# Wider rows for V and its attention outputs in a fused state-space and recurrent-memory kernel

## The chip, the cores and the metric

The kernel runs on one core of a Trainium2 chip. The metric is device time in microseconds (us) from start to end of one execution. Four runs of the kernel before gave a median of 1250.6 us, from 1249.58 to 1251.2. Lower is better. TensorE is written PE, VectorE DVE, ScalarE ACT, GpSimd POOL; SP is the engine that issues most DMAs.

## The reference

Two independent layers read two inputs of 2048 x 1024 and their outputs are joined on the last axis. Part A is a state-space layer, part B a transformer layer that walks over 64 segments of 32 tokens and carries 8 memory rows from one segment to the next:

```python
def _A_ref(...):
    Bu = jnp.einsum('bld,pd->blp', x + 0j, B_bar)
    for t in range(L):
        h = Lam_bar[None, :] * h + Bu[:, t, :]
    y = 2.0 * jnp.einsum('blp,dp->bld', hseq, Cmat).real + x * Dskip
def _B_ref(...):                       # H = 32 heads of Dh = 128, M = 8, seg_len = 32
    for s in range(n_seg):
        h = jnp.concatenate([mem, xs], axis=1)
        q, k, v = (einsum('btd,dhe->bhte', h, W) for W in (Wq, Wk, Wv))
        p = _softmax(where(mask, scores, -1e9))
        o = einsum('bhqk,bhke->bhqe', p, v)
        o = einsum('bhte,hed->btd', o, Wo)
        mem = o[:, :M, :]
        outs.append(o[:, M:, :])
```

(The sketch joins lines of the reference and leaves out its arguments.)

## The kernel before

The kernel does not walk over the 64 segments one by one. It makes a guess of every segment's memory rows (lines 517 to 536), computes all segments with that guess at once, and near the end checks the guess against the memory outputs that came out (`check`, lines 794 to 847). Only if the check fails would a loop over the segments (`general`) run; with the given inputs it does not.

The work runs in four stages, with TensorE kept supplied through all of them. Stage 1 (to about 347 us) computes part A's scan and, between its matmuls, V for all tokens. V is written from PSUM to two staging tiles `b_vst` by ACT (line 490, by the helper at L87) and from there to DRAM tensors `b_vx` (line 493), one for each block of 4 heads. V of the guessed memory rows goes to `b_vt` through `v_mem` (lines 539 to 557). Stage 2 (to about 471 us) computes part A's output and the guess. Stage 3 makes Q and K for a pair of heads at a time (`proj`) and does attention (`attention`) for the pair before, interleaved; its first scores come at 486.7 us and its last outputs at 1018 us. Stage 4 multiplies the attention outputs with Wo (`outproj`), with `check` between.

For attention, 64 segments are packed into 22 groups of 3; a group has 96 token rows and 3 memory rows, 99 in all. For each of 16 pairs of heads (`hp`) and each of 11 steps `u`, `att_front` makes scores for two groups and two heads (four matmuls of 128x99 into `psS`), ACT takes the exponential, and POOL multiplies with a 0/1 mask into `b_m` (line 642). `att_back` then takes up to three blocks at a time (a block is one group and one head). For each it loads the masked weights `b_m` into PE and streams V of that group and head past them (line 656):

```python
        for i, (_, b, m, j) in enumerate(blocks):
            PE.matmul(o[:, i, :], m[:, j * GW:j * GW + 128], vt[:, b // 2, (b % 2) * EV:(b % 2 + 1) * EV], start=True, stop=True)
```

V of a head has E = 128 columns and one more of ones, so that the same matmul gives the sum of the weights: EV = 129. In the tile `b_v` (called `vt` here) a group has 2 x 129 bf16 values, the second head directly after the first, and the three outputs of one PSUM tile lie 129 fp32 values apart. DVE then takes the reciprocal of the sums (line 658) and multiplies (line 659). In the trace the outputs are `psO` and, for every third tile, `psR`. There are 16 x 44 = 704 such matmuls.

`load_v` (lines 616 to 626) fills `b_v` for a pair of heads, from `b_vx` (96 rows x 22 groups, one run of 258 values each) and `b_vt`. For the first two pairs it also fills the unused partitions 99 to 127 with zeros (line 622), read from a zero row of `b_vx` for each of 29 partitions x 22 groups. `load_v(0)` is called when stage 3 is set up (line 688), the next ones at step `u == 2` of the pair before.

Every PE and SP instruction goes through the helper `Pinned` and therefore carries line L62 in the profile; ACT and DVE copies carry L87 and L89. In stage 1 PE and SP keep the order of the program, and SP in stage 2 too; in stages 3 and 4 the framework's scheduler may move instructions on SP forward. Tiles begin on multiples of 32 bytes. The constants' pool `cst` holds `b_omT` (5120 bytes a partition), the memory outputs transposed, which `check` reads (lines 800 to 811): four transposing DMAs fill it from `b_tn`.

Of the kernel before, what the change touches and what calls it, by code (L numbers as in the profile page):

```python
# [9 lines left out]
BF16 = mybir.dt.bfloat16  # L10
# [13 lines left out]
T = 2048; D = 1024; KC = 8; TT = 16  # L24
PC = 8; TB = 512; NB = 4
H = 32; E = 128; SEG = 32; M = 8; NSEG = 64; L = M + SEG
HB = 8; HP = 16
# [3 lines left out]
NG = 22; GX = 96; GW = 99; NU = NG // 2  # L31
NSLOT = NG * GX
QW = 2208
NTL = 3 * NG
NMX = 7
NM = NTL + NMX
NR = 80
GE = 6
EV = E + 1
MW = 4 * GW + 29  # L40

XMAIN = 1920
# [9 lines left out]
class Pinned:  # L52


    def __init__(self, k, name, eng):
        self.k, self.name, self.eng = k, name, eng
# [278 lines left out]
class PartB:  # L335
    def __init__(self, k, x, mem0, Wq, Wk, Wv, Wo, out):
        self.k = k
        self.x, self.mem0, self.out = x, mem0, out
        self.Wf = [w.rearrange("(c p) h e -> p c (h e)", p=128) for w in (Wq, Wk, Wv)]
        self.Wo = Wo.rearrange("h e d -> e h d")  # L340
        self.vx = [k.drp.tile([NSLOT, 4 * EV], BF16, name=f"b_vx{i}") for i in range(HB)]
        self.vt = [k.drp.tile([NTL, 4 * EV], BF16, name=f"b_vt{i}") for i in range(HB)]
        self.on = [k.drp.tile([T, 1024], BF16, name=f"b_on{i}") for i in range(4)]
        self.tn = [k.drp.tile([NR, 1024], BF16, name=f"b_tn{i}") for i in range(4)]
        c = k.cst
        self.m0T = c.tile([128, KC, M], BF16, name="b_m0T")
        self.omT = c.tile([128, H, NR], BF16, name="b_omT")
        self.gx = c.tile([128, KC, NM], BF16, name="b_gx")
        self.vmp = c
        self.xbar = c.tile([128, KC, NSEG], BF16, name="b_xbar")  # L350
        self.ogT = c.tile([128, H, NSEG], BF16, name="b_ogT")
        self.accE = c.tile([128, HP * NU], FP32, name="b_accE")
        self.accR = c.tile([128, HP * 2 * NG], FP32, name="b_accR")
        self.flag = c.tile([1, 1], I32, name="b_flag")
# [18 lines left out]

    def fill(self, tmp):
        k = self.k
        z = tmp.tile([32, 4 * EV], BF16, name="b_xr", bufs=4)
        k.V.memset(z[:], 0.0)
        for hb in range(HB):
            k.SP.dma_start(self.vx[hb][64 + NMX:GX, :], z[0:GX - 64 - NMX, :])
            k.SP.dma_start(self.vx[hb][T + 32:NSLOT, :], z[0:32, :])  # L380
        for q in range(4):
            k.SP.dma_start(self.tn[q][NM:NR, 0:4 * EV], z[0:NR - NM, :])
            k.SP.dma_start(self.tn[q][NM:NR, 1024 - 4 * EV:1024], z[0:NR - NM, :])

    def load_x(self, q):

# [60 lines left out]
    def stage_init(self):  # L447

        self.vst = []
        for i in range(2):  # L450
            self.vst.append(self.wl.tile([128, 4, 4, EV], BF16, name=f"b_vst{i}", bufs=1))
            self.k.G.memset(self.vst[i][:, :, :, E:EV], 1.0)
        self.nst = 0

    def next_st(self):
# [160 lines left out]
    def load_v(self, hp):  # L616
        if hp < HP:
            k = self.k
            vt = self.vts[hp % 2]
            if hp < 2:  # L620
                z = self.vx[0][T + 32:T + 32 + 128 - GW, 0:2 * EV].unsqueeze(1).to_broadcast([128 - GW, NG, 2 * EV])
                k.tc.keep_in_program_order(k.SP.dma_start(vt[GW:128, :, :], z))
            hb, cs = hp // 2, slice((hp % 2) * 2 * EV, (hp % 2) * 2 * EV + 2 * EV)
            k.tc.keep_in_program_order(k.SP.dma_start(vt[0:GX, :, :], self.vx[hb].rearrange("(g p) n -> p g n", p=GX)[:, :, cs]))
            k.SP.dma_start(vt[GX:GW, :, :], self.vt[hb].rearrange("(g j) n -> j g n", j=3)[:, :, cs])
            self.vtile[hp] = vt
# [19 lines left out]
    def att_back(self, blocks):  # L646

        k = self.k; PE, V = k.PE, k.V
        hp, b0, n = blocks[0][0], blocks[0][1], len(blocks)
        vt = self.vtile[hp]  # L650
        if b0 == 0:
            self.ob = self.p3a.tile([GW, 2 * NG, E], BF16, name="b_ob", bufs=2)
        o = k.ps(("O", "O", "R")[self.nback % 3], (128, 3, EV))
        self.nback += 1
        for i, (_, b, m, j) in enumerate(blocks):
            PE.matmul(o[:, i, :], m[:, j * GW:j * GW + 128], vt[:, b // 2, (b % 2) * EV:(b % 2 + 1) * EV], start=True, stop=True)
        r = self.accR[0:GW, hp * 2 * NG + b0:hp * 2 * NG + b0 + n]
        V.reciprocal(r, o[0:GW, 0:n, E])
        V.tensor_tensor(self.ob[:, b0:b0 + n, :], o[0:GW, 0:n, 0:E], r.unsqueeze(2).to_broadcast([GW, n, E]), ALU.mult)  # L659
        q, cs = hp // 4, slice((hp % 4) * 256, (hp % 4) * 256 + 256)  # L660
        on, tn = self.on[q], self.tn[q]
        ov = self.ob[:].rearrange("p (g h) e -> p g (h e)", h=2)
        early = hp == HP - 1

        def rows(g0, g1):
            r = on[64 + GX * (g0 - 1):64 + GX * (g1 - 1), :].rearrange("(g p) n -> p g n", p=GX)
            k.SP.dma_start(r[:, :, cs], ov[0:GX, g0:g1, :])
        if early and b0 + n == 2 * GE:
            rows(1, GE)
            k.SP.dma_start(on[0:64, cs], ov[0:64, 0, :])  # L670
        if b0 + n == 2 * NG:
            del self.vtile[hp]
            if early:
                rows(GE, NG - 1)
            else:
                rows(1, NG - 1)
                k.SP.dma_start(on[0:64, cs], ov[0:64, 0, :])
            k.SP.dma_start(on[T - 64:T, cs], ov[0:64, NG - 1, :])
            k.SP.dma_start(tn[0:NTL, :].rearrange("(g j) n -> j g n", j=3)[:, :, cs], ov[GX:GW, :, :])
            k.SP.dma_start(tn[NTL:NM, cs], ov[64:64 + NMX, 0, :])  # L680

    def att_init(self):
        self.vtile, self.nback = {}, 0
        self.mt = [self.p3a.tile([128, MW], BF16, name=f"b_m{i}", bufs=1) for i in range(5)]
        for m in self.mt:
            self.k.G.memset(m[:, 4 * GW:MW], 0.0)
            self.k.G.memset(m[96:128, 0:4 * GW], 0.0)
# [106 lines left out]
    def check(self):  # L794
        k = self.k; V, S, PE = k.V, k.S, k.PE
        pool = self.p4

        def small(name, n):
            return pool.tile([128, n], FP32, name=name, bufs=1)
        for q in range(4):  # L800
            k.SP.dma_start_transpose(self.omT[:, 8 * q:8 * q + 8, :], self.tn[q][:])
        yield
# [2 lines left out]
        for half in range(2):  # L805
            cs = slice(4 * half, 4 * half + 4)
            p = k.ps("P")
            for c in range(4):
                for h in range(H):
                    PE.matmul(p[:, c * NM:(c + 1) * NM], self.wo[half][:, h, c * 128:(c + 1) * 128], self.omT[:, h, 0:NM],  # L810
                              start=(h == 0), stop=(h == H - 1))
# [5 lines left out]
        ss = pool.tile([128, 2, NM], FP32, name="c_ss", bufs=1)  # L817
        V.tensor_reduce(ss[:], sq[:].rearrange("p a c n -> p a n c"), AX.X, ALU.add)
        onef = small("c_one", 1)
        V.memset(onef[:], 1.0)  # L820
        yield
        pd = k.ps("R")
        for i in range(2):
            PE.matmul(pd[0:NM, i:i + 1], ss[:, i, :], onef[:], start=True, stop=True)
        t2 = small("c_t2", 2)
        V.memset(t2[:], 0.0)
        V.tensor_copy(t2[0:NM, :], pd[0:NM, 0:2])
# [145 lines left out]
def kernel_main(tc, A_x, A_Lre, A_Lim, A_Bre, A_Bim, A_Cre, A_Cim, A_logdt, A_Dskip, B_x, B_mem0, B_Wq, B_Wk, B_Wv, B_Wo, out,  # L973
                force=False, dbg=None):
    with ExitStack() as ctx:
        k = K(tc, ctx)
# [3 lines left out]
        b = PartB(k, B_x, B_mem0, B_Wq, B_Wk, B_Wv, B_Wo, out)  # L980

        def pool(name, side, bufs=2):
            return tc.tile_pool(name=name, bufs=bufs, side=side, reuse_waits="tile")
# [105 lines left out]
        k.pin.clear()  # L1089
        p3 = ExitStack()  # L1090
        p3v = p3.enter_context(pool("p3v", "right"))
        b.vts = [p3v.tile([128, NG, 2 * EV], BF16, name=f"b_v{i}", bufs=1) for i in (1, 0)][::-1]
        b.p3a = p3.enter_context(pool("p3a", "right"))
        b.att_init()
        p3b = p3.enter_context(pool("p3b", "right"))
# [63 lines left out]
@with_exitstack  # L1159
def kernel(  # L1160
    ctx: ExitStack,
    tc: tile.TileContext,
    A_x: bass.AP,
    A_Lambda_re: bass.AP,
    A_Lambda_im: bass.AP,
    A_B_re: bass.AP,
    A_B_im: bass.AP,
    A_C_re: bass.AP,
    A_C_im: bass.AP,
    A_log_dt: bass.AP,  # L1170
    A_Dskip: bass.AP,
    B_x: bass.AP,
    B_mem0: bass.AP,
    B_Wq: bass.AP,
    B_Wk: bass.AP,
    B_Wv: bass.AP,
    B_Wo: bass.AP,
    B_seg_len: bass.AP,
    out: bass.AP,
):  # L1180
    assert int(B_seg_len) == SEG
    kernel_main(tc, A_x, A_Lambda_re, A_Lambda_im, A_B_re, A_B_im, A_C_re, A_C_im, A_log_dt, A_Dskip,
                B_x, B_mem0, B_Wq, B_Wk, B_Wv, B_Wo, out)
# [35 lines left out]
```

## Time and profile before

| | before |
|---|---|
| median of 4 runs | 1250.6 us |
| the profiled execution's own time | 1249.11 us |
| its span, first to last instruction | 1247.4 us |
| PE busy in the span | 1239.9 us, 99% |
| DVE, ACT, POOL busy | 668.1, 263.8, 276.1 us |
| granted PE clock | 0.999 |
| attention matmuls into psO and psR | 480 and 224 |
| DMA moved | 174.84 MB |

A row of the groups gives line, engine and operation, then what is written from what, the shapes, how many, the busy time of the group in us, and the mean of one in ns; the last number is the idle time ahead of them on their engine. Matmuls are pipelined: the mean of one (221 ns for 128x129) is the time from its start until its result is out, and the next starts long before. What a matmul costs in a stream of matmuls is therefore the distance from its start to the start of the next. "SPq" rows are the issue of a DMA by SP, with the time that SP needed for it, not the transfer.

### The profile page before, as it was taken

The numbers are of one execution on the slowest core, as the hardware profiler recorded it, in microseconds if no ns is written. First come the engines' busy times: TensorE is split into PE (matmuls) and PEld (weight loads), VectorE is DVE, ScalarE is ACT, GpSimd is POOL, SyncE is SP. The second block draws the span as 40 slices with busy tenths as digits, with TensorE's granted clock in tenths as the row PEclk, the third lists the DMA queues.
The fourth block names the chain that finished last, engine by engine and source line by source line (L and its number), as shares of the span: only waits on it lengthen the run. The fifth ranks groups of instructions, "written<-read, shape, count | busy, mean of one in ns | idle before, by whom it ended". The sixth has DMA issues, their size and how long they took to land.

```text
span 1247.4 us, 20193 instructions
## 1 busy us (share of the span) xinstructions
PE 1239.9 (99%) x8342; PEld 663.6 (53%) x8342; DVE 668.1 (54%) x1246; ACT 263.8 (21%) x631; POOL 276.1 (22%) x412
## 2 busy tenths in 40 slices
PE   9999999999999999999999999999999999999998
PEld 5444444444455555566666656555665554446444
DVE  4688899998711124666666666666666641001000
ACT  5344444443310000111212111111211110000000
POOL 3111331212332321322222222222222220000000
PEclk9999999999999999999999999999999999999999
DMA  9985444553898834765464545545374289407000
GB/s 242 236 225 144 128 134 128 138 150 109 236 320 249 247 114 91 205 151 122 90 147 106 142 106 113 140 90 133 93 159 93 57 224 215 99 18 153 17 17 27
DMA packets 316023, 174.84 MB, mean 140 GB/s; under 512 B 138651, under 2 KB 301327, under 8 KB 315927
## 3 DMA queue, kind: packets, MB, share of 16 engines
q1 hardware_dynamic: 293830, 146.88, 48.8%
q10 hardware_dynamic: 21072, 23.47, 5.9%
q0 software_dynamic: 1024, 3.17, 0.8%
q8 instruction: 66, 1.08, 0.4%
q14 instruction: 31, 0.25, 0.1%
HBM read 88.13 MB, written 52.19 MB: 112 GB/s over the span
## 4 chain that ended last, share of the span: by engine, by line
PE 99%; POOL 0%; ACT 0%; DVE 0%; issue 0%; ACTq 0%
PE psP L62 82%; PE psU L62 9%; PE psS L62 3%; PE psO L62 2%; PE psR L62 2%; POOL b_m L642 0%; ACT b_e L639 0%; DVE b_xe L89 0%; DVE b_ost L89 0%; DVE a_n L960 0%; ACTq L87 0%; ACTq L639 0%; DVE hpb L103 0%; DVE ones L100 0%
## 5 line engine op out<-in xcount | busy, mean ns | idle before, releaser
L62 PE MATMUL psP<-b_xe,b_wk 128*128 128x480 bf16 (+1 forms) x1280 | 247.6, 343 | 0.0
L62 PE MATMUL psP<-b_xe,b_wq 128*128 128x480 bf16 (+1 forms) x1280 | 247.6, 343 | 0.0
L62 PE MATMUL psP<-b_wv,b_xe 128*128 128x512 bf16 (+2 forms) x1048 | 224.4, 373 | 0.2 <-DVE b_xe L89 0.2
L642 POOL TENSOR_TENSOR b_m<-b_e,maskB 99x396 bf16<-99x396 bf16 x160 | 139.6, 873 | 335.4 <-ACT b_e L639 335.4
L639 ACT ACTIVATE b_e<-psS 99x396 bf16<-99x396 f32 x176 | 88.2, 501 | 534.0 <-PE psS L62 526.5
L62 PEld LDWEIGHTS <-b_wk 128*128 128x128 bf16 x1280 | 119.4, 98 | 94.2
L62 PEld LDWEIGHTS <-b_wq 128*128 128x128 bf16 x1280 | 118.8, 98 | 87.8
L62 PEld LDWEIGHTS <-b_xe 128*128 128x128 bf16 x1056 | 101.8, 98 | 119.2 <-DVE b_xe L89 0.4
L89 DVE CAST b_k<-psP 128x480 bf16<-128x480 f32 (+1 forms) x192 | 98.1, 532 | 101.7 <-PE psP L62 101.7
L89 DVE CAST b_q<-psP 128x480 bf16<-128x480 f32 (+1 forms) x192 | 98.1, 532 | 93.8 <-PE psP L62 92.0
L62 PEld LDWEIGHTS <-b_ol 128*128 128x128 bf16 x864 | 84.3, 98 | 94.4
L62 PE MATMUL psU<-a_xT,a_bt 128*128 128x512 bf16 x512 | 114.9, 379 | 0.0
L62 PE MATMUL psP<-t,a_hl 128*128 128x512 bf16 x512 | 113.1, 379 | 0.0
L89 DVE CAST b_ost<-psP 128x512 bf16<-128x512 f32 (+1 forms) x17 | 11.5, 676 | 183.4 <-PE psP L62 183.4
L62 PE MATMUL psP<-wo,b_ol 128*128 128x512 bf16 (+1 forms) x448 | 92.5, 364 | 0.0
L62 PE MATMUL psP<-t,b_ol 128*128 128x512 bf16 x416 | 92.2, 379 | 0.0
L278 POOL TENSOR_SCALAR a_tt<-a_pr,a_tabf 128x1 f32<-128x1 f32 x48 | 34.1, 710 | 243.5 <-DVE a_pr L273 243.5
L87 ACT ACTIVATE b_vst<-psP 128x512 bf16<-128x512 f32 x126 | 72.5, 592 | 69.1 <-PE psP L62 63.0
L659 DVE TENSOR_TENSOR b_ob<-psO,b_accR 99x384 bf16<-99x384 f32 x160 | 85.8, 553 | 2.2
L265 DVE TENSOR_TENSOR a_pr<-psU,a_tabf 128x2048 f32<-128x2048 f32 x32 | 73.0, 2282 | 16.2 <-PE psU L62 16.1
L62 PEld LDWEIGHTS <-a_bt 128*128 128x128 bf16 x512 | 49.2, 98 | 57.6
L62 PEld LDWEIGHTS <-a_hl 128*128 128x128 bf16 x512 | 49.0, 98 | 56.7
(199 smaller groups left out, 965.8 us busy)
## 6 DMA issues: line engine op xcount, KB each, us to landing
b_v<-b_vx SPq DMA_DIRECT2D x16, 1064.2 KB
b_wv<-in_B_Wv_dram SPq DMA_DIRECT2D x16, 1024.0 KB
b_on<-b_ob SPq DMA_DIRECT2D x15, 960.0 KB
b_vx<-b_vst ACTq DMA_DIRECT2D x24, 516.0 KB
a_hs<-a_h SPq DMA_DIRECT2D x32, 256.0 KB
b_wog<-in_B_Wo_dram SPq DMA_DIRECT2D x4, 2048.0 KB
b_wq<-in_B_Wq_dram SPq DMA_DIRECT2D x16, 512.0 KB
b_wk<-in_B_Wk_dram SPq DMA_DIRECT2D x16, 512.0 KB
```

The costliest lines, as they stand in the source:

```text
L62: r = f(*a, **kw)
L87: self.S.activation(out, in_, ACT.Copy)
L89: self.V.tensor_copy(out, in_)
L265: V.tensor_tensor(pr[:], u[:].unsqueeze(1).to_broadcast([128, 2, 2, TB]), view(t3, [[TB + 1, 2], [TB + 1, 2], [1, TB]]), ALU.mult)
L278: G.tensor_scalar(tt[:, j:j + 1], w[:, j, TB - 1:TB], t3[:, 1, TB:TB + 1], None, ALU.mult)
L639: k.S.activation(e[:], s[0:GW], ACT.Exp, scale=float(E) ** -0.5, accum_out=self.accE[0:GW, i:i + 1])
L642: k.G.tensor_tensor(m[0:GW, 0:4 * GW].rearrange("p (a b q) -> p a b q", a=2, b=2), e[:], mask[0:GW, :, :].unsqueeze(2).to_broadcast([GW, 2 ...
L659: V.tensor_tensor(self.ob[:, b0:b0 + n, :], o[0:GW, 0:n, 0:E], r.unsqueeze(2).to_broadcast([GW, n, E]), ALU.mult)
```

## The change

The head's pitch in V becomes EW = 136 columns, 272 bytes: in the staging tiles, in the DRAM tensors `b_vx` and `b_vt`, and in `b_v`. The matmul still streams 129 columns; the 7 others hold ones and are read by nobody. The PSUM pitch becomes EO = 132 fp32 values, 528 bytes. The DMA runs of V become 544 and 1088 bytes in place of 516 and 1032. `b_omT` leaves `cst` and is allocated in the pool `p4`, which opens after attention. As built, no instruction on PE, DVE, ACT or POOL changes its place; on SP, three of the four transposing DMAs into `b_omT` go from the attention stage (642.72, 777.90 and 923.30 us in the trace of before) to the place of the fourth (1067.53 us), and the load of Wk for one pair is issued three DMAs earlier.

```diff
+EW = E + 8
+EO = E + 4
...
-        self.vx = [k.drp.tile([NSLOT, 4 * EV], BF16, name=f"b_vx{i}") for i in range(HB)]
-        self.vt = [k.drp.tile([NTL, 4 * EV], BF16, name=f"b_vt{i}") for i in range(HB)]
+        self.vx = [k.drp.tile([NSLOT, 4 * EW], BF16, name=f"b_vx{i}") for i in range(HB)]
+        self.vt = [k.drp.tile([NTL, 4 * EW], BF16, name=f"b_vt{i}") for i in range(HB)]
...
-        self.omT = c.tile([128, H, NR], BF16, name="b_omT")
...
-        z = tmp.tile([32, 4 * EV], BF16, name="b_xr", bufs=4)
+        z = tmp.tile([32, 4 * EW], BF16, name="b_xr", bufs=4)
...
-            k.SP.dma_start(self.tn[q][NM:NR, 0:4 * EV], z[0:NR - NM, :])
-            k.SP.dma_start(self.tn[q][NM:NR, 1024 - 4 * EV:1024], z[0:NR - NM, :])
+            k.SP.dma_start(self.tn[q][NM:NR, 0:4 * EW], z[0:NR - NM, :])
+            k.SP.dma_start(self.tn[q][NM:NR, 1024 - 4 * EW:1024], z[0:NR - NM, :])
...
-            self.vst.append(self.wl.tile([128, 4, 4, EV], BF16, name=f"b_vst{i}", bufs=1))
-            self.k.G.memset(self.vst[i][:, :, :, E:EV], 1.0)
+            self.vst.append(self.wl.tile([128, 4, 4, EW], BF16, name=f"b_vst{i}", bufs=1))
+            self.k.G.memset(self.vst[i][:, :, :, E:EW], 1.0)
...
-                z = self.vx[0][T + 32:T + 32 + 128 - GW, 0:2 * EV].unsqueeze(1).to_broadcast([128 - GW, NG, 2 * EV])
+                z = self.vx[0][T + 32:T + 32 + 128 - GW, 0:2 * EW].unsqueeze(1).to_broadcast([128 - GW, NG, 2 * EW])
...
-            hb, cs = hp // 2, slice((hp % 2) * 2 * EV, (hp % 2) * 2 * EV + 2 * EV)
+            hb, cs = hp // 2, slice((hp % 2) * 2 * EW, (hp % 2) * 2 * EW + 2 * EW)
...
-        o = k.ps(("O", "O", "R")[self.nback % 3], (128, 3, EV))
+        o = k.ps(("O", "O", "R")[self.nback % 3], (128, 3, EO))
...
-            PE.matmul(o[:, i, :], m[:, j * GW:j * GW + 128], vt[:, b // 2, (b % 2) * EV:(b % 2 + 1) * EV], start=True, stop=True)
+            PE.matmul(o[:, i, 0:EV], m[:, j * GW:j * GW + 128], vt[:, b // 2, (b % 2) * EW:(b % 2) * EW + EV], start=True, stop=True)
...
+        self.omT = pool.tile([128, H, NR], BF16, name="b_omT", bufs=1)
         for q in range(4):
             k.SP.dma_start_transpose(self.omT[:, 8 * q:8 * q + 8, :], self.tn[q][:])
...
-        b.vts = [p3v.tile([128, NG, 2 * EV], BF16, name=f"b_v{i}", bufs=1) for i in (1, 0)][::-1]
+        b.vts = [p3v.tile([128, NG, 2 * EW], BF16, name=f"b_v{i}", bufs=1) for i in (1, 0)][::-1]
```

## The prediction

> **What bounds the kernel now.** I read the page first (busy times, chain, granted clock), then the groups by shape in the attention stage, then single steps in the timeline, and last SP's rows around the start of attention.
>
> ```profile
> PE 1239.9 (99%) x8342; PEld 663.6 (53%) x8342; DVE 668.1 (54%) x1246; ACT 263.8 (21%) x631; POOL 276.1 (22%) x412
> ...
> PEclk9999999999999999999999999999999999999999
> ...
> PE 99%; POOL 0%; ACT 0%; DVE 0%; issue 0%; ACTq 0%
> ```
>
> PE is never free and runs at full clock; the chain that ended last is PE alone. Time goes away only where PE has less to do, or where one of its few waits shrinks. A cheaper DVE, ACT or DMA is worth nothing by itself. Being busy does not prove that each matmul goes at its best rate, so the next view is the attention stage by shape (all engines' stretches from 486 to 1018 us, PE alone):
>
> ```profile
> L62 PE MATMUL psS<-b_q,b_k 128*128 128x99 bf16 x704 | 60.1, 208 | 0.0
> L62 PE MATMUL psO<-b_v,b_m 128*128 128x129 bf16 x480 | 49.5, 221 | 1.1 <-POOL b_m L642 0.8 <-issue 0.2
> L62 PE MATMUL psR<-b_v,b_m 128*128 128x129 bf16 x222 | 25.8, 221 | 0.0
> ```
>
> The change touches the 480 + 224 matmuls of 128x129 (the window cuts two off). Their 221 ns is latency; the rate is read from starts. One step in the timeline:
>
> ```profile
> 704.63 0.34 PE L62 MATMUL psS<-b_q,b_k 128*128 128x99 bf16 x4
> 704.81 0.34 PE L62 MATMUL psO<-b_v,b_m 128*128 128x129 bf16 x3
> 704.99 0.34 PE L62 MATMUL psR<-b_v,b_m 128*128 128x129 bf16 x3
> 705.16 0.25 PE L62 MATMUL psP<-b_xe,b_wq 128*128 128x201 bf16 x1
> ```
>
> Six matmuls of 129 columns take 705.16 - 704.81 = 0.35 us, 58 ns each. PE does not wait between them.
>
> The last view is the load of V for the first pair of heads:
>
> ```profile
> 465.74 0.25 SPq L62 DMA_DIRECT2D b_v<-b_vt  x1
> 466.04 16.49 SPq L62 DMA_DIRECT2D b_v<-b_vx  x2
> 482.57 4.05 SPq L62 DMA_DIRECT2D b_wq<-in_B_Wq_dram  x1
> ...
> 491.87 0.34 PE L62 MATMUL psS<-b_q,b_k 128*128 128x99 bf16 x4
> 492.40 0.36 PEld L62 LDWEIGHTS <-b_m 128*128 128x128 bf16 x6 [0.34 <-issue]
> 492.43 0.46 PE L62 MATMUL psO<-b_v,b_m 128*128 128x129 bf16 x5 [0.22 <-issue]
> ```
>
> The two DMAs at 466.04 are the zero fill (29 partitions x 22 runs = 638) and the real load (96 x 22 = 2112 runs). The second held SP until 482.53. Then the stretches:
>
> ```profile
> 469.00:482.00 13.00, 13.00 (x84) 7.65 (x83) 5.79 (x26) 0.00 (x0) 0.00 (x0) 1.00 0.13 41
> 484.00:487.00 3.00, 3.00 (x19) 1.55 (x18) 1.07 (x3) 0.00 (x0) 0.00 (x0) 1.00 1.16 234
> ```
>
> From 469 to 482 us DMA is 0.13 busy and part of that is stores of part A's output: the zero fill runs on one DMA engine of 16. Only then does the real load go at full width. Its 16th part, on that engine, lands at 492.34 by the trace's landing events, the other 15 by 490.42. PE's last scores start at 492.00, a next matmul could start 44 ns later, and the first output matmul starts at 492.43: about 0.38 us of PE is lost here, and the load's landing sets it exactly.
>
> **The change, part by part.**
>
> 1. *The 704 matmuls, SBUF side.* I took all their starts from the trace and joined them with the byte at which V begins (tiles begin on multiples of 32, so it is 516 x group + 258 x head, modulo 16). Three are held by POOL's mask at the end of attention; of the other 701:
>  96 begin on a multiple of 16: 56.2 ns to the next start (55 to 66).
>  605 do not: 59.2 ns (55 to 68); by offset 2, 4, 6, 8, 10, 12, 14 the means are 59.0, 58.7, 59.7, 58.9, 59.0, 59.1, 59.9.
> With 272 bytes a head and 544 a group every one begins on 16. That saves 605 x (59.2 - 56.2) = 1.8 us, all of it on PE's path. Bounds: nothing, if what the 96 have in common is something else, and 704 x 3 = 2.1 us.
>  Two rules of the Trainium skill speak against this. "SBUF — State Buffer", § Specifications, gives 16-byte cachelines and a penalty for each crossing to a new line. 258 bytes touch 17 lines from any even offset, 0 or 14 alike, and so by that rule the saving is 0 and the kernel stays at 1250.6. The rows of equal line count differ by 3 ns, so I go by the rows. "TensorE: Matmul & The Clock Gate", § Back-to-back issue gap, puts a stream of LDWEIGHTS and MATMUL pairs at N=128 at about 81 ns, which would leave the weight load as the limit and again save 0. This trace has 58 at N=129 with a new LDWEIGHTS for each, so the weight load isn't the limit.
>
> 2. *PSUM pitch 528.* The 96 aligned ones cost 56.3, 56.3 and 56.0 ns with outputs beginning at 0, 4 and 8 bytes modulo 16; the 605 cost 57.9, 60.2 and 59.5. So the pitch is worth nothing once V is aligned, and I add 0. DVE's reads (553 ns for 99x384, L659) may change either way; DVE is 302 of 478 us busy from 530 to 1008 and PE never waits for it there. Without that cover a nanosecond in each of the 240 reads would cost 0.2 us.
>
> 3. *Longer DMA runs.* Everything of V grows by 5.4%. Stores to `b_vx` and `b_vt` and later loads of `b_v` are hidden: V of the second pair is loaded from 491.82, with the same 16.67 us of zero fill, and its first use is some 30 us later. The first load is not hidden. The slow engine has 638 + 132 = 770 runs, and 16.11 us for 638 is 25.3 ns a run. What does a run of 544 bytes take in place of 516? In the trace's DMA records the commonest times are 18 ns for 256 bytes, 27 for 512, 28 for 516, 46 for 1024, 47 for 1032. From 512 to 1024 it is 19 ns for 512 bytes, 1.2 ns for 32; but 4 bytes beyond 512 cost 1, and 8 beyond 1024 cost 1. So time goes in steps of about 32 bytes, 516 and 544 both fill 17 of them, and the change is 0. Bounds: +1.0 ns a run if it goes by bytes, 770 x 1.0 = +0.8 us; on the good side the 0.38 us that PE waits now, no more. I take 0, by the rows nearest in size, 512 to 516.
>
> 4. *`b_omT`.* Its 4 transposes (1.24 to 1.28 us each on SP) now stand together near 1067.5 us. Three more delay the four stores of outputs behind them by 3.8 us; PE waits for no store. Moved past are also the loads that follow, the next of which issues at 1122.81 because it waits for a buffer. The matmuls that read `b_omT` start at 1129.5, nearly 60 us later. The tile now lies on memory that `b_ob` had, whose last DMA is issued by 1025.6. In the attention stage SP loses three rows of 1.3 us, for nothing: 0. With that cover gone the price would be at most 4 x 1.3 = 5 us.
>
> 5. *The rest.* The ones in the staging tiles: 8 columns each for POOL (174 to 203 ns for 128x16 before; 0.20 us for the 128x128 of L96 at 0.82), perhaps +0.1 us ahead of the iota that ends at 5.25, which DVE reads at 6.37: 0. The load of Wk three DMAs earlier around 515 us: no PE wait there: 0.
>
> Sum: 1247.4 - 1.8 = 1245.6 for the span; the profiled execution lies at 1249.11, 1.7 us around the span, and goes to 1247.3. It is 1.5 below the median of the runs shown, so the median goes from 1250.6 to 1248.8, 0.14%. A measurement of this kernel can tell about 0.2% (2.5 us) from no change; the runs of before alone spread over 1.6 us.
>
> **The rivals.**
>
> *B, runs pay by the byte.* The wait at 492 us grows from 0.38 to 1.2: -1.8 + 0.8, 1249.6. For it: the fill is one engine at its own pace, fully exposed. Against: the step from 512 to 516.
>
> *C, a little more than the rows.* The load lands early and the 0.38 us goes too, and the matmuls take 56.0 ns, the lowest of the aligned means, which is 0.1 more: 1248.3, and with the luck of the runs under 1248.1.
>
> *D, the matmuls don't change.* Every eighth block happens to be aligned, and something else about it, not the alignment, makes it quick: 1250.6. Against: aligned ones stand at all three places of an output tile, 32 at each, at the same 56.
>
> *E, slower.* One mechanism: the 544-byte run, which is no whole number of 64, is handled as 512 + 32. A run of 512 takes 27 ns and the shortest records (4 bytes) 9, so a run would take some 36 in place of 28. On the exposed engine that is 770 x 8 = 6.2 us at 492 us, against 1.8 gained: 1255.0. It decides from 1.8 / 0.77 = 2.3 ns a run and makes the kernel slower by over 0.2% from 5.6 ns. Nothing in the trace shows a split; 516 and 1032 are single records.
>
> **How the numbers follow.** Main case 0.60, B 0.16, C 0.12, D 0.06, E 0.06. Two medians of a few runs each may be off by some 0.7 us against each other. The main case alone gives 1248.0 to 1249.6. For 8 in 10 the range reaches to B and D above and C below with that scatter: 1247.3 to 1250.6. Under 1248.1 (faster by over 0.2%) lies about a fifth of the main case and most of C: 0.24. Slower is E and a little scatter: 0.07. Within 0.2% is the rest: 0.69.
>
> **What would show it.** In the profile of the changed kernel, six matmuls into psO and psR should take 0.34 us start to start in place of 0.35, every start 56 ns apart whichever group and head; psS, psP and their counts stay. The chain stays PE 99%. SP's zero fill should again hold the next DMA for about 16.1 us (16.8 in case B, over 20 in E), and the first psO should start near 492.4. The transposes into `b_omT` stand together at about 1067 us and the matmuls that read them start with no idle time. The prediction is wrong if starts stay at 59 ns, if the first psO comes more than 1 us later, or if PE has a new idle time at 1129.

## The result, and the profile after

The changed kernel takes 1247.83 us (median of 34 runs, 1247.27 to 1248.59); the kernel before, on the same chip, 1249.80 (54 runs, 1248.56 to 1253.83). The ratio is 0.9982, 95% interval 0.9978 to 0.9987: 0.18% less time, just inside what the prediction called no difference that can be told. A second comparison, with the last experiments, gave 1247.55 beside 1249.69, ratio 0.9979 (0.9970 to 0.9988). Forecast were 1248.8 beside 1250.6, a ratio of 0.9986. So the forecast of the time held. The reason given for it did not, as the experiments show.

The profiled execution has a span of 1245.7 us in place of 1247.4, at a granted clock of 0.999. From the page of the changed kernel (busy time and count of each engine, then the chain that ended last):

```profile
PE 1237.8 (99%) x8342; PEld 662.1 (53%) x8342; DVE 667.8 (54%) x1246; ACT 263.1 (21%) x631; POOL 276.1 (22%) x412
...
PEclk9999999999999999999999999999999999999999
...
PE 99%; DMA 0%; POOL 0%; ACT 0%; issue 0%; DVE 0%; SPq 0%; ACTq 0%
```

PE has the same 8342 matmuls, is as full as before, and still carries the whole chain; it is 2.1 us less busy. L62 of before is L64 here, and L642 is L643. The attention stage by shape, PE alone, 486 to 1018 us:

```profile
L64 PE MATMUL psS<-b_q,b_k 128*128 128x99 bf16 x704 | 60.1, 208 | 0.0
L64 PE MATMUL psO<-b_v,b_m 128*128 128x129 bf16 x480 | 48.6, 220 | 0.9 <-POOL b_m L643 0.9
L64 PE MATMUL psR<-b_v,b_m 128*128 128x129 bf16 x224 | 25.7, 220 | 0.0
```

psS has not moved (60.1 us). psO went from 49.5 to 48.6 us busy with the same count, and its idle time lost the 0.2 us put down to "issue", which belong to the wait at 492. The row of psR can't be compared, since the window now takes in two more of them. The same step as before in the timeline (start, duration, engine, and how many instructions the row holds):

```profile
703.78 0.34 PE L64 MATMUL psS<-b_q,b_k 128*128 128x99 bf16 x4
703.96 0.33 PE L64 MATMUL psO<-b_v,b_m 128*128 128x129 bf16 x3
704.13 0.33 PE L64 MATMUL psR<-b_v,b_m 128*128 128x129 bf16 x3
704.30 1.55 PE L64 MATMUL psP<-b_xe,b_wq 128*128 128x201 bf16 x16
```

Six matmuls take 704.30 - 703.96 = 0.34 us, where it was 0.35. And the first load of V:

```profile
465.71 0.25 SPq L64 DMA_DIRECT2D b_v<-b_vt  x1
466.01 16.18 SPq L64 DMA_DIRECT2D b_v<-b_vx  x2
482.24 4.13 SPq L64 DMA_DIRECT2D b_wq<-in_B_Wq_dram  x1
...
491.84 0.34 PE L64 MATMUL psS<-b_q,b_k 128*128 128x99 bf16 x4
492.06 0.35 PEld L64 LDWEIGHTS <-b_m 128*128 128x128 bf16 x6
492.09 0.50 PE L64 MATMUL psO<-b_v,b_m 128*128 128x129 bf16 x6
```

SP is held by the load behind the zero fill for 16.18 us in place of 16.49. The first psO starts 0.25 us after the scores' row where it was 0.56; 0.18 is what it takes with no wait at all (as in the step at 703.78).

I laid the two traces side by side, each of the 8342 matmuls against the same one. The order on PE is identical, so that every start-to-start time has its counterpart:

| part | before to after, us |
|---|---|
| psO, 480 matmuls | -1.05 |
| psR, 224 matmuls | -0.45 |
| wait at 492 us | -0.31 |
| behind the last matmul | -0.13 |
| psP of 480 columns | +0.17 |
| first 9 us (arrival of the first loads) and rest | +0.05 |
| span | -1.7 |

The 701 output matmuls that nothing holds went from 41.21 us to 39.67 in sum, from 58.78 to 56.60 ns each (from the start of one to the start of the next). That is 1.53 us before rounding, most of the 1.7; the shorter wait at 492 is the next largest part.

### The profile page after: what moved, and what is told of

The parts are those of the page before. It is cut to its first block, busy times and chain, and to the rows that moved or that the text cites. A ratio compares the mean times of both kernels' runs of the same rounds, so it can differ in the third digit from the quotient of the medians.

```text
span 1245.7 us, 20192 instructions
## 1 busy us (share of the span) xinstructions
PE 1237.8 (99%) x8342; PEld 662.1 (53%) x8342; DVE 667.8 (54%) x1246; ACT 263.1 (21%) x631; POOL 276.1 (22%) x412
## 3 DMA queue, kind: packets, MB, share of 16 engines
q0 software_dynamic: 1024, 3.17, 0.7%
## 4 chain that ended last, share of the span: by engine, by line
PE 99%; DMA 0%; POOL 0%; ACT 0%; issue 0%; DVE 0%; SPq 0%; ACTq 0%
PE psP L64 82%; PE psU L64 9%; PE psS L64 3%; PE psO L64 2%; PE psR L64 2%; DMA b_xr<-in_B_x_dram 0%; POOL b_m L643 0%; ACT b_e L640 0%; ACT b_xe L89 0%; DVE b_ost L91 0%; SPq L64 0%; ACTq L89 0%; ACTq L640 0%
## 5 line engine op out<-in xcount | busy, mean ns | idle before, releaser
L64 PE MATMUL psP<-b_xe,b_wq 128*128 128x480 bf16 (+1 forms) x1280 | 247.7, 343 | 0.0
L64 PE MATMUL psP<-b_xe,b_wk 128*128 128x480 bf16 (+1 forms) x1280 | 247.7, 343 | 0.0
L64 PE MATMUL psP<-b_wv,b_xe 128*128 128x512 bf16 (+2 forms) x1048 | 224.5, 372 | 0.2 <-ACT b_xe L89 0.2
L643 POOL TENSOR_TENSOR b_m<-b_e,maskB 99x396 bf16<-99x396 bf16 x160 | 139.4, 871 | 334.7 <-ACT b_e L640 334.7
L64 PEld LDWEIGHTS <-b_wk 128*128 128x128 bf16 x1280 | 119.4, 98 | 94.2
L64 PEld LDWEIGHTS <-b_wq 128*128 128x128 bf16 x1280 | 118.7, 98 | 87.7
L64 PEld LDWEIGHTS <-b_xe 128*128 128x128 bf16 x1056 | 101.9, 98 | 119.1 <-ACT b_xe L89 0.3
L64 PEld LDWEIGHTS <-b_ol 128*128 128x128 bf16 x864 | 84.3, 98 | 94.4
L64 PE MATMUL psU<-a_xT,a_bt 128*128 128x512 bf16 x512 | 114.9, 379 | 0.0
L64 PE MATMUL psP<-t,a_hl 128*128 128x512 bf16 x512 | 113.1, 379 | 0.0
L64 PE MATMUL psP<-wo,b_ol 128*128 128x512 bf16 (+1 forms) x448 | 92.5, 364 | 0.0
L64 PE MATMUL psP<-t,b_ol 128*128 128x512 bf16 x416 | 92.2, 379 | 0.0
L64 PEld LDWEIGHTS <-a_bt 128*128 128x128 bf16 x512 | 49.2, 98 | 57.6
L64 PEld LDWEIGHTS <-a_hl 128*128 128x128 bf16 x512 | 49.0, 98 | 56.7
```

What stands on the lines that cost most here:

```text
L64: r = f(*a, **kw)
L643: k.G.tensor_tensor(m[0:GW, 0:4 * GW].rearrange("p (a b q) -> p a b q", a=2, b=2), e[:], mask[0:GW, :, :].unsqueeze(2).to_broadcast([GW, 2 ...
```

## The experiments

Each was timed beside the kernel before, whose medians were 1249.53, 1249.64 and 1249.69 us in three groups of experiments. A ratio is to the kernel before, with its 95% interval.

**One part each: V's pitch, PSUM's pitch, the start of V on 16 bytes, `b_omT`.** The first takes the new PSUM pitch out of the changed kernel:

```diff
-EO = E + 4
+EO = EV
```

> V has 136 columns a head as in the changed kernel, but PSUM rows stay at 129 values. If the start of V on 16 bytes is all that counts (my theory), the 701 unheld output matmuls again take about 56.6 ns start to start (39.7 us together, against 41.2 before), the first psO starts near 492.1, and the ratio to before is 0.9980 to 0.9986. If the PSUM pitch has a part in it, outputs at 4 and 8 bytes modulo 16 take 58 ns or more, the sum is 40.4 us or more and the ratio 0.9988 or more.

Measured: 1247.93 us, ratio 0.9983 (0.9976 to 0.9989). The output matmuls take 39.67 us in sum, 56.60 ns each, whatever the PSUM byte. The gain in the matmuls is all there without the PSUM pitch.

The second puts only the PSUM pitch into the kernel before:

```diff
+EO = E + 4
-        o = k.ps(("O", "O", "R")[self.nback % 3], (128, 3, EV))
+        o = k.ps(("O", "O", "R")[self.nback % 3], (128, 3, EO))
-            PE.matmul(o[:, i, :], m[...
+            PE.matmul(o[:, i, 0:EV], m[...
```

> V stays at 129 columns, PSUM rows are 132 values. In the trace of before the 605 unaligned matmuls took 57.9 ns with outputs at 0 modulo 16, 60.2 at 4 and 59.5 at 8. If these three differ by the PSUM byte, all go to about 57.9, the sum from 41.2 to 40.4 us, and the ratio is about 0.9993. If they differ by their place in the group of three, and the PSUM byte is idle (my theory: the pitch is worth nothing), the sum stays at 41.2 us and the ratio within 0.0003 of 1. The first psO stays at 492.4 in both.

Measured: 1249.16 us, ratio 0.9995 (0.9987 to 1.0004); 41.20 us in sum, 58.78 ns each, as before. With outputs now all on 16 bytes, the first, second and third matmul of a PSUM row still take 57.7, 59.7 and 59.0 ns. The differences by PSUM byte that the prediction listed are differences by place in the row.

The third shifts V in the changed kernel by four columns, so that every output matmul begins 8 bytes past a multiple of 16:

```diff
+VO = 4
-            k.copy("v" if first and i % 2 else "s", st[:, i, :, 0:E], ...
+            k.copy("v" if first and i % 2 else "s", st[:, i, :, VO:VO + E], ...
...
-            PE.matmul(o[:, i, 0:EV], m[:, j * GW:j * GW + 128], vt[:, b // 2, (b % 2) * EW:(b % 2) * EW + EV], start=True, stop=True)
+            PE.matmul(o[:, i, 0:EV], m[:, j * GW:j * GW + 128], vt[:, b // 2, (b % 2) * EW + VO:(b % 2) * EW + VO + EV], start=True, stop=True)
```

> The changed kernel, with each head's values in columns 4 to 132 of its 136, so that V begins 8 bytes past a multiple of 16. DMA runs, pitches and PSUM rows are those of the changed kernel. By my theory all 704 are unaligned: 58 to 59 ns each, 40.7 to 41.5 us together, and the first psO still near 492.1, so the ratio to before is 0.9995 to 1.0000. If pitch, run length or PSUM rows bring the saving, it stays at 56.6 ns, 39.7 us and 0.9982.

Measured: 1247.69 us, ratio 0.9983 (0.9976 to 0.9989). The sum is 39.72 us, 56.66 ns each, with not one on 16 bytes. The 80 blocks 8 bytes off took 58.9 ns in before. My theory of the start on 16 bytes fell here: the pitch brings the gain, but not by the alignment of the start.

The fourth moves only `b_omT`, in the kernel before:

```diff
-        self.omT = c.tile([128, H, NR], BF16, name="b_omT")
...
+        self.omT = pool.tile([128, H, NR], BF16, name="b_omT", bufs=1)
```

> Only the transposed memory outputs move to the last pool; V and PSUM rows as before. My theory: their DMAs move to about 1067 us on SP and nothing waits for them, the ratio is within 0.0003 of 1, the output matmuls stay at 41.2 us and the first psO at 492.4. Rival: the three transposes leave the attention stage and the earlier load of Wk gives PE something, or the readers at 1129 wait: a ratio outside 0.9995 to 1.0005.

Measured: 1249.72 us, ratio 1.0002 (0.9993 to 1.0011), output matmuls 41.21 us. No gain or loss from it can be told.

**A new theory, from the same trace of before.** What had the quick blocks in common, if not the start? With 129 columns a head, the blocks of V lie end to end, 258 bytes apart, and PE reads them one after the other. A block that starts on a multiple of 16 is the only one whose first 16 bytes do not also hold the last bytes of the block before it. So I sorted the 701 matmuls of before anew, by whether the matmul just ahead of it on PE had ended in the same 16 bytes:

| in the trace of before | matmuls | ns to the next start |
|---|---|---|
| begins in the 16 bytes where the one before ended | 462 | 59.84 |
| all others | 239 | 56.75 |
| of these: not on 16 bytes, but behind a score matmul | 143 | 57.11 |

All 462 of the first row take 59 ns or more. The third row could have been read before the prediction: of these 143 blocks, which start off the 16 bytes with a psS (once a psP) between them and their neighbour, 111 are quick (56.40 ns). The other 32, blocks 12 and 30 (counted from 0) of every pair of heads, take 59 or 60 without a shared line: a smaller slow class that comes back below. Three experiments test this "line" theory against two others.

The first leaves every byte where it is in the kernel before, and only turns the order of the three matmuls of a PSUM row:

```diff
-        for i, (_, b, m, j) in enumerate(blocks):
+        for i, (_, b, m, j) in reversed(list(enumerate(blocks))):
```

> The kernel before, V pitch 129 and all, with one change: the three output matmuls of a PSUM row are issued last block first. Theory L (line): in the trace of before, 462 of the 701 unheld output matmuls follow a matmul that ended in the very 16 bytes in which they begin (the next head of V, 258 bytes on), and these take 59.84 ns start to start; the other 239 take 56.75. What costs is reading a 16-byte line that the matmul just before has just read. Reversed, no matmul begins where its predecessor ended: all 701 at 56.6 to 56.8, sum 39.7 us in place of 41.2, the run at 1248.0 against 1249.5 of before, without a byte of V moved. Theory A (the start of V on its own bytes, whatever was read before it) and theory N (heads of V that touch in memory, whatever the order): the addresses are those of before, so the mean stays at 58.8, the sum at 41.2 and the run at 1249.5.

Measured: 1248.74 us, ratio 0.9991 (0.9983 to 0.9999). The output matmuls take 40.05 us, 57.06 ns each (702 of them, since one more is free of waits), in place of 41.21 and 58.78. That is most of what the line theory forecast, but not the whole (39.7 us). The same kind of step in the timeline of this kernel:

```profile
705.61 0.34 PE L62 MATMUL psS<-b_q,b_k 128*128 128x99 bf16 x4
705.79 0.33 PE L62 MATMUL psO<-b_v,b_m 128*128 128x129 bf16 x3
705.96 0.34 PE L62 MATMUL psR<-b_v,b_m 128*128 128x129 bf16 x3
706.13 1.55 PE L62 MATMUL psP<-b_xe,b_wq 128*128 128x201 bf16 x16
```

Six in 706.13 - 705.79 = 0.34 us, at V's old addresses. Alignment and touching heads are the same as in before, so neither can be the cause of what was gained here; the order alone brings about 1.2 of the 1.53 us. The run gained less than that (0.9 us by the medians): the last three rows of attention, which wait for POOL's mask, now begin with the block whose mask is last, and PE's three waits there are 1.76 us start to start where they were 1.52. The forecast of 1248.0 us was missed by 0.7.

The second takes 132 columns a head in the changed kernel:

```diff
-EW = E + 8
+EW = E + 4
```

> The changed kernel with 132 columns of V a head (264 bytes) in place of 136: even blocks begin on 16 bytes, odd ones 8 behind, and an odd block's first 16 bytes hold its even neighbour's last two. Theory L: 304 of the 704 output matmuls begin in the line where the one before ended and cost 59.8, the others 56.6: mean 58.0, sum 40.6 us, the run about 1248.7 to 1249. Theory A in the form that 8 bytes are enough (with 8 bytes off all were quick): all at 56.6, sum 39.7, 1247.9. Theory N (a gap between heads is what counts): as A.

Measured: 1248.24 us, ratio 0.9988 (0.9982 to 0.9995), sum 40.62 us, mean 57.94 (expected 40.6 and 58.0). By the trace, 301 matmuls begin where the one before ended and take 60.22 ns; the other 400 take 56.23. Among these are 48 odd blocks, 8 bytes off, that come behind a score matmul: 56.35. The gap between one block's end and the next one's start is 6 bytes everywhere, and only where it lies inside one 16-byte line is the next matmul slow. That excludes the gap, and the start, as causes. It also fixes the size of the line. Of the 400 quick ones, 113 begin in the same 32 bytes (but not the same 16) in which the one before ended, and take 56.05, so 32 is not the unit. The 301 slow ones begin in the upper 8 bytes of a line and the one before ended in the lower 8, so 8 is not the unit either.

The third takes 137 columns, so that the starts go through all even offsets, but no two blocks share a line:

```diff
-EW = E + 8
+EW = E + 9
```

> The changed kernel with 137 columns of V a head (274 bytes): the starts go through all even offsets from 16 bytes as in before, but 16 bytes lie between the end of one head and the start of the next, so no two share a line. Theory L: all 701 at 56.6, sum 39.7 us, about 1247.9. Theory A in any form (starts on 4, 8 or 16 bytes are quick): seven of eight, or half, of the starts are off, and these at 59: mean 57.8 to 58.8, sum 40.5 to 41.2. Theory N: 56.6, as L.

Measured: the output matmuls take 39.96 us, 57.01 ns each, 1.25 under before; those on 16 bytes take 56.66, the others 57.06. The theory holds here too, but not to the last tenth (39.7 us were forecast): 133 of the 701 still take 59 ns or more, nearly all where V starts 8, 12 or 4 bytes past a multiple of 16 (64 of 80, 48 of 80 and 20 of 96). In the reversed order it is 129 of 702, nearly all at 14, 10 and 12 bytes. No block in either kernel shares a line with its predecessor. The same class is in before (the 32 above) and in the kernel with V 8 bytes off (47, all behind a score matmul). It takes the same block numbers in nearly every pair of heads. A block's number also fixes where its mask starts in `b_m`, so V's start alone need not be what matters. What makes this smaller class slow, some 0.4 us in all, stays open; in the changed kernel it does not occur.

The run did not gain: 1249.98 us, ratio 1.0004 (0.9994 to 1.0014). Its profiled execution took 1251.55 us, 1.6 more than the median, and has three longer waits of PE. One belongs to the zero fill; SP's rows:

```profile
468.25 17.14 SPq L64 DMA_DIRECT2D b_v<-b_vx  x2
485.44 4.69 SPq L64 DMA_DIRECT2D b_wq<-in_B_Wq_dram  x1
```

The fill took 17.14 us in place of 16.18, for runs of 548 bytes in place of 544: 0.96 us over 638 runs is 1.5 ns a run for 4 bytes, where 28 bytes more (516 to 544) had cost nothing. This row scatters, from 16.13 to 16.64 over all kernels with runs of 516 to 544 bytes; against the longest of these it is still 0.8 ns a run. The DMA records agree: the commonest time is 28 ns for 516 and for 544 bytes, 29 for 548. The wait at 492 grew by 1.29 us against before, as much as the matmuls had gained. Two other waits of PE, at 33.8 us (+1.72) and at 344.7 (+0.56), belong to an earlier part; the one at 33.8 also stands in the reversed order (+1.30), where V's rows are those of before, so I don't put it down to the pitch.

**The wait at 492 us.** The fill of V's 29 spare partitions runs on one DMA engine. In the changed kernel I let it fill 32, three of which are loaded again behind it:

```diff
-                z = self.vx[0][T + 32:T + 32 + 128 - GW, 0:2 * EW].unsqueeze(1).to_broadcast([128 - GW, NG, 2 * EW])
-                k.tc.keep_in_program_order(k.SP.dma_start(vt[GW:128, :, :], z))
+                z = self.vx[0][T + 32:T + 64, 0:2 * EW].unsqueeze(1).to_broadcast([32, NG, 2 * EW])
+                k.tc.keep_in_program_order(k.SP.dma_start(vt[96:128, :, :], z))
```

> The changed kernel with the zero fill of V's spare partitions widened from 29 partitions (99 to 127) to 32 (96 to 127; the three more are written again by the load behind it), which should spread its runs over all 16 DMA engines instead of one. In the changed kernel the fill takes 16.1 us on one engine, and the load behind it lands its last part at 492.0, where PE waits some 0.1 us for it. If the fill is spread (some 704 runs of 25 ns over 16 engines, about 1.1 us and the fixed cost of a transfer), the load is done by about 480 and nothing waits at 492: 0.1 us or less quicker, 1247.6 to 1247.9, no difference that can be measured. If the fill stays on one engine, 0.8 us later than now: 1248.6.

Measured: 1247.36 us, ratio 0.9974 (0.9966 to 0.9983). V was expected to be there by about 480 us, and was not. SP's rows in this kernel:

```profile
471.09 0.39 SPq L64 DMA_DIRECT2D t<-in_B_Wo_dram  x1
471.53 11.89 SPq L64 DMA_DIRECT2D b_v<-b_vx  x2
490.68 0.24 SPq L64 DMA_DIRECT2D b_v<-b_vt  x1
...
493.05 4.60 SPq L64 DMA_DIRECT2D b_v<-b_vx  x2
```

A load of Wo, 4096 runs of 1024 bytes, now stands ahead of V's fill; the changed kernel issues it at 518.61. Two stretches of this kernel (busy us and count for each engine, then granted clock, DMA share, GB/s):

```profile
469.00:482.00 13.00, 13.00 (x84) 7.65 (x83) 5.50 (x26) 0.00 (x0) 0.00 (x0) 1.00 0.77 253
484.00:487.00 3.00, 3.00 (x19) 1.54 (x18) 1.08 (x3) 0.00 (x0) 0.00 (x0) 1.00 1.18 257
```

From 469 to 482 us DMA is 0.77 busy, where it is 0.13 in the changed kernel, but by the DMA records that is mostly the load of Wo: the first run of V's fill starts at 484.62. The fill and the loads of V, 2882 runs, then end by 495.72. On one engine the fill's 704 runs alone would take 17.8 us at the 25.3 ns of before, so the fill is spread over more than one. The second pair shows it too: there fill and load hold SP for 4.60 us. In the changed kernel they hold it for 18.46:

```profile
489.15 18.46 SPq L64 DMA_DIRECT2D b_v<-b_vx  x2
```

PE's wait at 492 is gone, but not because V comes sooner: its last run ends at 495.72 us, and at 490.88 in the changed kernel. In this kernel the scheduler has put projections ahead of the first psO, which starts at 497.44 in place of 492.09:

```profile
497.06 0.34 PE L64 MATMUL psS<-b_q,b_k 128*128 128x99 bf16 x4
497.24 0.37 PE L64 MATMUL psP<-b_xe,b_wk 128*128 128x480 bf16 x1
497.44 0.50 PE L64 MATMUL psO<-b_v,b_m 128*128 128x129 bf16 x6
```

No PE row there has idle time. At 492.09 V would not have been there, so it is the later use that took the wait away. What the wide fill would do with all else in its place, no run here shows.

The same edit alone in the kernel before, and together with the reversed order:

> The kernel before with the zero fill of V's spare partitions widened from 29 partitions to 32, so that its runs go over 16 DMA engines (in the changed kernel this took the wait of PE at 492 away). Theory: the 0.38 us at 492 in before are the price of the fill on one engine and nothing else hangs on it: the wait goes to nothing, the output matmuls stay at 41.2 us in sum (mean 58.8), the run 0.4 us quicker, 1249.1 to 1249.3 beside 1249.6 of before: no difference that can be measured. Rival: the wait at 492 covers another late transfer (the next weights), which then holds PE as long: the wait stays at 0.3 us or more.

Measured: 1249.24 us, ratio 1.0000 (0.9990 to 1.0010). The wait at 492 went from 0.38 us to nothing, the output matmuls stayed at 41.21 us and 58.79 ns, and no wait of PE came in its place in attention. Here too the load of Wo goes ahead of the fill and the first psO comes only at 497.40, so this does not show that the fill was the price of the 0.38 us. The time is not measurably different, as expected of 0.4 us; the profiled span is even 0.1 longer, because the waits of PE in the first 9 us, which scatter from one execution to the next, took 0.5 us more.

> The kernel before, V pitch 129, with the two edits that move no tile: output matmuls of a PSUM row last block first, and the zero fill over 32 partitions. Theory L and the fill add up: output matmuls 40.05 us in sum as in the reversed order alone (mean 57.06, none of them beginning in the line where the one before ended), no wait at 492: 1.2 + 0.4 = 1.6 us under before, 1248.0 beside 1249.6. If the gain of the reversed order was chance (its run came with an interval of 0.9983 to 0.9999), 1249.2.

Measured: 1248.00 us, ratio 0.9989 (0.9980 to 0.9998); output matmuls 40.05 us, no wait at 492. By the median it is what was expected, by the interval it is somewhere from 0.2 to 2.5 us under before. So the gain of the reversed order came a second time, with the output matmuls' sum the same to 0.01 us; the wide fill adds nothing that can be told.

Last, the changed kernel once more, and with the wide fill, on one chip:

> The changed kernel as it is, beside the one with the fill over 16 engines on the same chip: 1.5 us of output matmuls and some 0.3 us at 492 under before: 1247.8 beside 1249.6.

> The changed kernel with the zero fill over 32 partitions, once more, beside the changed kernel on the same chip: the wait left at 492 in the changed kernel is about 0.07 us, so 0.1 us quicker than that, no difference that can be measured (within 0.2%); its sum of output matmuls 39.7 us, no wait at 492.

Measured: 1247.55 us (ratio 0.9979, 0.9970 to 0.9988) for the changed kernel, 1247.48 (0.9982, 0.9973 to 0.9991) with the wide fill. The output matmuls take 39.67 and 39.68 us. The wait at 492 is 0.19 and nothing. No version beats the changed kernel, timed beside it, by anything that can be measured.

## Why the prediction was right, and where it was not

*What bounds it.* Right. PE alone sets the end, before and after, and the gain is what the matmuls and the one wait gave. That the sum came out so near has luck in it: the matmuls gave 1.53 us where 1.8 were forecast, and the wait, which was put at nothing, gave 0.31.

*Step 1, the SBUF side: the number held, the cause did not.* The saving was put at 605 x 3.0 = 1.8 us on the ground that a start on 16 bytes is quick and any other slow. The saving is 1.53, and it is not the start. What failed is the sorting. I sorted by the byte of each block and not by what the matmul before it had read, and in before the two nearly coincide, because blocks of 258 bytes lie end to end: a start on 16 bytes is just where no line is shared. The 143 unaligned blocks behind a score matmul are the ones where they part, and they were averaged into the 605. With the new sorting the sum is 462 x (59.84 - 56.60) = 1.50, and 239 x (56.75 - 56.60) = 0.04 for the rest, as measured. The 239 hold the 32 of the smaller slow class, which the change did away with as well. The quick rate was 56.6 and not 56.2. That is not because the 96 blocks are special: the same 96 take 56.70 in the changed kernel, where they took 56.21. Why all quick ones went up by some 0.4 ns is open.

The two rules weighed against the change. "SBUF — State Buffer", § Specifications, speaks of 16-byte lines. I took from it a count of lines per matmul, 17 either way, and rightly did not let it stop the forecast. But the line of 16 bytes is the unit that matters, where two successive matmuls meet in one: in the kernel with 132 columns, the same 6 bytes of gap cost 60.22 - 56.23 = 4.0 ns inside a line and nothing across one. The back-to-back gap of "TensorE: Matmul & The Clock Gate", § Back-to-back issue gap, for LDWEIGHTS and MATMUL pairs (81 ns at N=128) is again not what bounds here: 56.6 ns.

*Step 2, PSUM pitch.* Right at 0, shown both ways: taking it out of the changed kernel leaves 56.60, putting it alone into before leaves 58.78.

*Step 3, longer runs.* Right at 0 for the runs: SP's row is 16.18 us in place of 16.49, and 28 bytes more cost nothing, while the 4 bytes beyond 544 cost 0.8 to 1.5 ns a run. That fits the steps of about 32 bytes that the prediction read from the records: 544 bytes fill 17 of them, 548 begin the next. So B (by the byte) and E (a split) are out. The wait itself went from 0.38 to 0.07 us, a part of C. How much of that is the change isn't settled. In profiled executions with 129 or 132 columns the first psO starts 0.56, 0.18, 0.74, 0.68 and 0.68 us after its scores, with 136 columns 0.25, 0.31, 0.41 and 0.37: shorter on the whole, but within the scatter, and the 0.18 (only the PSUM pitch changed) is no wait at all.

*Step 4, `b_omT`.* Right at 0. The transposes stand together, PE reads the tile 60 us later and shows no idle time, and moved alone they change nothing that can be told (1.0002):

```profile
1065.25 5.21 SPq L64 DMA_TRANSPOSE b_omT<-b_tn  x4
...
1127.92 2.26 PE L64 MATMUL psP<-b_omT,t 128*128 128x73 bf16 x62
```

*Step 5* cost nothing that shows: the first 9 us differ by less than they do between two executions of one kernel.

*Rival D* was nearer to the truth than its chance of 0.06 in one half: something other than the alignment of the start made every eighth block quick. It went wrong in the other half, that the change would then do nothing. The wider pitch removed the true cause along with the supposed one.

## What to carry to other kernels

Where a stream of short matmuls reads one operand block after block, see that a block does not begin in the 16 bytes in which the one read just before it ended: pad the pitch to a multiple of 16 bytes, or, if memory is short, change the order so that a block does not follow the neighbour that ends where it begins, which brought about 1.2 of 1.53 us here with no byte moved. Sort start-to-start times by what precedes as well as by the instruction's own address before believing in an alignment; two properties that coincide in one layout are told apart by one experiment that shifts everything by half a unit. Check the size of DMA runs at the step as well: 516 to 544 bytes was free, 548 was not. And when one DMA is changed, read the order of all around it: here a wider fill let a load of Wo go ahead of it, and a busy DMA share that looked like the fill was that load.

## What the runs showed of the hardware that was not expected

- A 128x129 matmul whose moving operand begins in the 16-byte line where the one before it ended takes 59.8 ns to the next start (129 columns) or 60.2 (132 columns), in place of 56.2 to 56.8. The unit is 16 bytes, neither 8 nor 32.
- A start 8 bytes past a line costs next to nothing by itself: 56.66 ns for 701 matmuls, with 56.60 on the line.
- Without any shared line, 133 (137 columns), 129 (reversed order), 47 (V 8 bytes off) and 32 (before) of some 700 matmuls still took 59 ns or more, at certain block numbers. The cause stays open.
- With a zero fill of 29 partitions DMA was 0.13 busy from 469 to 482 us, and the second pair's fill and load held SP for 18.46 us; with one of 32 partitions they held it for 4.60.
- A fill of 638 runs on one DMA engine held SP for 16.13 to 16.64 us at 516 to 544 bytes and for 17.14 at 548; the commonest record is 28 ns at 516 and 544 bytes and 29 at 548.
